# A weight ring of five chunks, a later load of key and value, and four chunks moved, in an attention and two-layer MoE kernel

## The chip, the cores and the metric

The kernel runs on one core of a Trainium2 chip. The metric is the time of one execution on the device in microseconds (us). The core has TensorE (PE, matmuls), VectorE (DVE), ScalarE (ACT), GpSimd (POOL, here only an issuer of DMAs) and SyncE (SP, the main issuer of DMAs). Each takes its own instructions in a fixed order, so an instruction that waits holds up all that stand behind it on its engine.

## The reference

```
a     = softmax over m of phi                     # phi: 4 batches, 8 heads, 576 tokens, 32 memories
k_m   = a^T k ;  v_m = a^T v                      # 32 memories of 64 per head
attn  = softmax(q k_m^T / 8) v_m                  # per head; then heads side by side: 512 per token
h     = relu(x @ w_in)                            # layer 1: 512 -> 2048
y     = (h * h) @ w_out                           # 2048 -> 512
h2    = y @ w_in2                                 # layer 2: 512 -> 2048
out   = (h2 * tanh(softplus(h2))) @ w_out2        # 2048 -> 512
```

There are 2304 tokens, 576 in each of 4 batches. The four weight matrices come in as 64-bit floats.

## The kernel before, in words

**Weights.** A *chunk* is 128 rows of 512 weights as pairs of 32-bit words, 512 KB. It is converted on the core: a Prelu on ACT works on the high words (line 197 in layer 1, 295 in layer 2), then a shift and a merge on DVE (lines 213 and 215, or 312 and 314) make 32-bit floats. Most operands are then split into a rounded *high* part (ACT) and the rest, the *low* part (DVE), and each product takes three matmuls: high by high, low by high, high by low. Layer 1 has 32 chunks (`i1` for w_in, `o1` for w_out, class `Conv`), layer 2 also 32 (`i2`, `o2`, class `Fold`).

**Conv.** `order` is the list of layer 1's chunks. `load` issues a chunk's load on SP into a raw tile that `spots` names: chunks 0 to 17 use nine places, six of them lent by other tiles, from chunk 18 on three. Ten chunks are begun in a script written out by hand at the start (line 659 on, with `strict(True)`: every engine keeps the order of the program). After that `tick` is called once per f: it begins one chunk on ACT, makes the bits of the one begun a tick ago, and the high and low parts of the one before it. `bits` calls `load` for a later chunk, when its raw tile is done with. `after` names the instruction behind which the DVE part is ordered; where it is set, that part is also behind the last emptying of a sum (`marks["ys"]`).

**Layer 1.** v_m is multiplied into w_in once per batch, so that layer 1 works on the softmax's weights: 32 matmuls of 64 rows (line 514) make two *pages* of the product, `wp`; for batches 2 and 3 w_in comes back from DRAM (`load_page`, line 947). `a_tile` (line 600) is the main loop: for one half batch of 288 tokens and a range of f (16 blocks of 128 of the 2048), six matmuls make h (lines 613 to 615), ACT takes ReLU and square (624, 625), ACT or DVE the high part (629, 631), DVE the low part (632), and, three f later, twelve matmuls add into four sums in PSUM (575 to 577). After the last f, `evac_y1` empties the sums (590, 592, 594). One f is 18 matmuls. Batches 0 and 1 are done in three groups of f, 0 to 3, 4 to 7, 8 to 15, each for four half batches (`subs`, numbered 0 to 11; 0 and 1 are in the script), because the weights arrive meanwhile. Then come batch 2's halves and batch 3's halves with all 16 f each.

**Fold.** Layer 2 is computed with seven products for eight; `Fold` makes their operands from pairs of chunks: per pair two Prelu, two shifts, two merges, four sums and seven casts (ACT high, line 331; DVE low, 332), each of which POOL stores (333). `fold.tick` begins a chunk every second or third f and takes one step of a pair, two where more than four wait. `fold.cap` (26, `EARLY`) is how many chunks are taken before batch 3; what is left of them is run off in a `while fold.busy()` loop after batch 2, and the rest goes to batch 3's f. The cast tiles rotate over the idle places of other tiles: first over that of k and v (`kv`, as `parts`), in batch 3 over those (`ru`) that later take layer 2's operands.

**Key and value.** k and v of one half of the heads are one tile with one buffer (`kv`). `kv_unit` makes the memories in five steps; after the first two, `kv_later` leaves n idle f (1 for batch 2), in which the next k and v land.

**Order.** Where no `issue_after` or `behind` binds, a planner with its own model of times sets the order on each engine, mostly by the program's order.

Of the kernel before, what the change touches and what calls it, by code (L numbers as in the profile page):

```python
# [18 lines left out]
P = 128  # L19
# [13 lines left out]
ROLE = [0, 1, 2, 3, 0, 2, 3]  # L33
EARLY = 26

# [22 lines left out]
def body(tc, q, kvm, kvt, phi, w_in1, w_out1, w_in2, w_out2, out):  # L58
# [41 lines left out]
    kv_t, kt_t, q_t = {}, {}, {}  # L100

    def load_phi(b, p):
        sp.dma_start(phi_t[p][:, at[p]:at[p] + S], phi[b, p])

    def load_kv(b, p):

        t = Y.tile([P, 2, 4, NC, D], F32, tag="kv", name=f"kv{b}{p}", bufs=1)
        sp.dma_start(
            t.rearrange("p s g c d -> p s (g c d)"), kvm[b, p].rearrange("s p x -> p s x"))
        kv_t[b, p] = t  # L110
# [49 lines left out]

    marks = {}

    @contextlib.contextmanager
# [8 lines left out]
    class Conv:  # L172


        def __init__(self, order, spot, ready=lambda key, u: True):
            self.order, self.spot, self.ready = list(order), spot, ready
            self.loaded = self.started = 0
            self.limit, self.after, self.paced, self.hold = len(self.order), None, False, False
            self.raw, self.flight, self.done = {}, [], set()

        def load(self, n=1):
            for _ in range(n):
                if self.loaded == len(self.order):
                    return
                key, u = self.order[self.loaded]
                pool, tag, bufs = self.spot(self.loaded)
                t = pool.tile([P, 512, 2], I32, tag=tag, name=f"raw_{key}_{u}", bufs=bufs)
                src = w_v[key][u] if key[0] == "i" else w_v[key][:, u, :]
                sp.dma_start(t.rearrange("p o t -> p (o t)"), src)
                self.raw[key, u] = t  # L190
                self.loaded += 1
# [9 lines left out]
        def bits(self, x, place=None):  # L201
# [16 lines left out]
            if key == "i1" and c:  # L218
                nc.gpsimd.dma_start(w1[u // 2], wt["i1", u // 2])
            self.raw.pop((key, u))  # L220
            if not self.hold:
                self.load()
# [42 lines left out]
    class Fold:  # L265


        def __init__(self, order):
            self.order = list(order)
            self.cap = len(self.order)  # L270
            self.loaded = self.started = 0
            self.raw, self.bits, self.odd, self.steps = {}, [], {}, []
            self.pool, self.stage, self.n = None, None, 0

# [14 lines left out]
        def tick(self, start=True):  # L289
            todo, self.bits = self.bits, []  # L290
            if start and self.started < self.loaded and len(self.steps) < 5:
                key, u = self.order[self.started]
                high = self.raw[key, u][:, :, 1].bitcast(F32)
                with behind(marks, "step"):
                    act.activation(high, high, AF.Prelu, scale=2.0 ** -112, alpha=-2.0 ** 32)
                self.started += 1
                self.bits.append((key, u))
            with behind(marks, "step"), behind(marks, "low"), behind(marks, "ys"):
                for key, u in todo:
                    self.fields(key, u)  # L300
                for _ in range(2 if len(self.steps) > 4 else 1):
                    if self.steps:
                        self.steps.pop(0)()
# [277 lines left out]
    def evac_y1(b, half, first, last):  # L581
        slot = 2 * b + half if b < 2 else half

        def f(dm, o):
# [6 lines left out]
            elif dm % 2 == 0:  # L591
                act.copy(st, o)
            else:
                marks["ys"] = vec.tensor_copy(st, o)
# [52 lines left out]
    for f0, f1 in zip(bounds, bounds[1:]):  # L647
# [4 lines left out]
        for f in range(f0, f1, 2):  # L652
            order.append(("o1", f))
            if f + 2 < f1:
                order += [("i1", f + 2), ("i1", f + 3)]
            order.append(("o1", f + 1))
    spots = [(Y, "raw", 3)] * 3 + [
        (wo, f"wo{part}{j}", 1) for j in (7, 6, 5) for part in "hl"]

    c1 = Conv(order, lambda i: spots[i % 9 if i < 18 else i % 3],  # L660
              lambda key, u: key != "i1" or u < 8 or (1, u // 2 - 4) in wp)
# [99 lines left out]
    bits(1)  # L761
    first_h(0, 0)
    ps = banks2("pw001")[:, :, :P]
    w_mm([ps[:, p] for p in range(2)], 0, 0, P, 2 * P)
    act.copy(plain[0][:, :, P:], ps)
    relu(0, 0)
# [92 lines left out]
    first_a(1, 3)  # L859
    first_y(1)  # L860
    bits(9)
    c1.low(conv[6])
    c1.low(conv[7])
    strict(False)
# [7 lines left out]
    def kv_later(b):  # L872
# [10 lines left out]

        n = 1 if b == 2 else 4
        return [[u, 2], [iter(range(n)), n], [u, 3]]

    def counted(u, counts):
        for n in counts:
            for _ in range(n):
                next(u)  # L890
            yield

# [57 lines left out]
    for i, (f0, f1, b, half) in enumerate(subs):  # L950
# [3 lines left out]
        if i == 2:  # L954
            c1.after, c1.paced = "first", True
            lanes = [[counted(at11, (2, 1, 2)), 3]]
        elif i == 3:
            drain(lanes)
            c1.after = (1, 1)
        elif i == 4:  # L960
            c1.after = None
        elif i == 8:
# [3 lines left out]
        elif final:  # L966
            drain(lanes)
            lanes = [[iter(range(2)), 2]] + attn_later(2, 0)
            for j in range(4):
                load_page(j)  # L970

        def tick(fc):
            if len(c1.done) < 2 * NF:
                c1.tick(start=(i, fc) != (2, 0))

# [86 lines left out]
    cm_cv, CV = open_pool("cv", "right")  # L1062
    fold.pool = CV
    def stage_cv(n):
# [321 lines left out]
```

## Time and profile before

| | us |
|---|---|
| median of 3 runs | 744.89 |
| lowest, highest | 744.54, 745.78 |
| profiled execution, whole | 745.91 |
| profiled execution, span | 744.1 |
| PE, DVE, ACT busy | 726.7 (98%), 524.0 (70%), 419.7 (56%) |
| chain that ended last | PE 83%, DMA 8%, DVE 4%, ACT 3% |

The span is what the profiler saw between the first and the last instruction. An engine's busy time is the time in which at least one of its instructions ran; matmuls overlap, so a busy PE is not PE at its peak. Idle time of PE is what can be saved, as far as nothing else takes its place. The granted clock of PE is full throughout.

### The profile page before, as it was taken

What the parts mean: (1) busy time and instruction counts of PE and PEld (TensorE: products, weight loads), DVE (VectorE), ACT (ScalarE), POOL (GpSimd) and SP (SyncE); (2) the same over time, 40 slices, a digit from 0 to 9 for tenths busy, and PEclk for the clock granted to TensorE, in tenths of its full rate; (3) what the DMA queues carried; (4) which work ended last, traced back from release to release, by engine and by line L of the source; (5) the groups of instructions that cost most, each with busy time, mean ns of one, the idle gap of its engine ahead of it and who ended that gap; (6) DMA issues with size and microseconds to landing.
All of it is one profiled execution on the core that took longest, in us unless ns stands there. A gap on an engine that the chain in (4) does not pass through costs nothing.

```text
span 744.1 us, 16262 instructions
## 1 busy us (share of the span) xinstructions
PE 726.7 (98%) x5990; PEld 696.5 (94%) x5990; DVE 524.0 (70%) x1117; ACT 419.7 (56%) x957; POOL 66.7 (9%) x128
## 2 busy tenths in 40 slices
PE   8998998999999999999999999999999999999998
PEld 7677997998989989899999999999999999999998
DVE  4879867655777798969556767955667873666574
ACT  3767867774777687857435336533435552434552
POOL 0000000221212232424100000000000000000000
PEclk9999999999999999999999999999999999999999
DMA  8994554589898588767829889898978788778882
GB/s 331 406 353 142 199 168 144 204 300 343 281 333 303 192 294 302 281 244 269 306 90 331 258 289 322 262 293 272 315 248 268 244 289 267 271 230 270 248 267 71
DMA packets 89327, 195.33 MB, mean 262 GB/s; under 512 B 9888, under 2 KB 22688, under 8 KB 89248
## 3 DMA queue, kind: packets, MB, share of 16 engines
q1 hardware_dynamic: 78992, 160.60, 64.3%
q0 software_dynamic: 10112, 33.56, 11.8%
q8 instruction: 48, 0.79, 0.4%
q14 instruction: 31, 0.25, 0.1%
q10 hardware_dynamic: 144, 0.13, 0.1%
HBM read 151.26 MB, written 42.99 MB: 261 GB/s over the span
## 4 chain that ended last, share of the span: by engine, by line
PE 83%; DMA 8%; DVE 4%; ACT 3%; issue 1%; SPq 1%; DVEq 0%; ACTq 0%
PE hb L1186 8%; PE hb L1187 8%; PE hb L1188 8%; PE a L575 6%; PE a L577 6%; PE a L576 6%; DMA raw_o<-in_moe_w_out_dram 3%; PE h L613 3%; PE h L614 3%; PE h L615 3%; DMA raw_i<-in_moe_w_in_dram 2%; PE a L53 2%; DMA kv<-in_kvm_dram 1%; DMA kv01v<-in_kvm_dram 1%; PE h L53 1%
## 5 line engine op out<-in xcount | busy, mean ns | idle before, releaser
L575 PE MATMUL a<-g,o1h 128*128 128x288 f32 x480 | 140.6, 298 | 5.5 <-DVE ys L590 3.6
L576 PE MATMUL a<-g,o1l 128*128 128x288 f32 x480 | 139.3, 295 | 0.0
L577 PE MATMUL a<-g,o1h 128*128 128x288 f32 x480 | 128.6, 297 | 0.6 <-DVE g L632 0.6
L1187 PE MATMUL hb<-ycl,u 128*128 128x384 f32 x336 | 112.9, 336 | 0.0
L1186 PE MATMUL hb<-ych,u 128*128 128x384 f32 x336 | 112.9, 336 | 0.0
L1231 DVE TENSOR_TENSOR opl<-a,oph 128x384 fp32r<-128x384 f32 x144 | 79.1, 556 | 45.3 <-ACT oph L1230 44.7
L1188 PE MATMUL hb<-ych,u 128*128 128x384 f32 x336 | 109.4, 336 | 0.0
L1230 ACT CAST oph<-a 128x384 fp32r<-128x384 f32 x144 | 73.9, 513 | 58.8 <-PE b20b L1254 7.0
L575 PEld LDWEIGHTS a<-g,o1h 128*128 128x128 f32 x480 | 90.2, 188 | 9.2 <-DVE ys L590 3.5
L1192 ACT ACTIVATE a<-hs 128x384 f32<-128x384 f32 x72 | 37.8, 526 | 97.4 <-DVE hs L1196 97.4
L576 PEld LDWEIGHTS a<-g,o1l 128*128 128x128 f32 x480 | 90.4, 188 | 0.2 <-issue 0.2
L577 PEld LDWEIGHTS a<-g,o1h 128*128 128x128 f32 x480 | 85.6, 188 | 1.7 <-DVE g L632 1.3
L624 ACT ACTIVATE s<-h 128x288 f32<-128x288 f32 x120 | 49.1, 410 | 60.9 <-PE h L615 55.9
L613 PE MATMUL h<-ah,wp 128*128 128x288 f32 x240 | 72.8, 304 | 1.7 <-ACT s L624 0.8
L614 PE MATMUL h<-al,wp 128*128 128x288 f32 x240 | 70.9, 296 | 0.5 <-DVE al L506 0.5
L632 DVE TENSOR_TENSOR g<-s,g 128x288 fp32r<-128x288 f32 x120 | 54.3, 453 | 23.7 <-ACT g L629 22.7
L615 PE MATMUL h<-ah,wp 128*128 128x288 f32 x240 | 70.6, 296 | 0.0
L1196 DVE TENSOR_TENSOR hs<-hu,hb 128x384 f32<-128x384 f32 x72 | 39.8, 553 | 41.1 <-PE hb L1188 40.5
L1186 PEld LDWEIGHTS hb<-ych,u 128*128 128x128 f32 x336 | 63.1, 188 | 0.0
L1187 PEld LDWEIGHTS hb<-ycl,u 128*128 128x128 f32 x336 | 63.0, 188 | 0.0
L1188 PEld LDWEIGHTS hb<-ych,u 128*128 128x128 f32 x336 | 62.8, 188 | 0.0
L625 ACT ACTIVATE s<-s 128x288 f32<-128x288 f32 x120 | 52.9, 446 | 0.9
(358 smaller groups left out, 1707.4 us busy)
## 6 DMA issues: line engine op xcount, KB each, us to landing
u<-wf_i SPq DMA_DIRECT2D x168, 256.0 KB, 4.0
u<-wf_o SPq DMA_DIRECT2D x168, 256.0 KB, 3.3
raw_i<-in_moe_w_in_dram SPq DMA_DIRECT2D x32, 512.0 KB, 6.6
raw_o<-in_moe_w_out_dram SPq DMA_DIRECT2D x32, 512.0 KB, 5.3
wf_i<-st POOLq DMA_DIRECT2D x41, 256.0 KB, 4.5
wf_o<-st POOLq DMA_DIRECT2D x39, 256.0 KB, 4.6
win1r<-w_i SPq DMA_DIRECT2D x16, 512.0 KB, 6.3
kv<-in_kvm_dram SPq DMA_DIRECT2D x5, 1024.0 KB, 6.9
```

The costliest lines, as they stand in the source:

```text
L575: pe.matmul(o, wh[:, c, cs], sh, start=first, stop=False)
L576: pe.matmul(o, wl[:, c, cs], sh, start=False, stop=False)
L577: done_pe["main"] = pe.matmul(o, wh[:, c, cs], sl, start=False, stop=last)
L613: pe.matmul(ph, w[:, 0, hg, fs], hi[:, hg], start=(hg == 0), stop=False)
L614: pe.matmul(ph, w[:, 0, hg, fs], lo[:, hg], start=False, stop=False)
L615: done_pe["h"] = pe.matmul(ph, w[:, 1, hg, fs], hi[:, hg], start=False, stop=(hg == 1))
L632: marks["low"] = vec.tensor_sub(sl, s, sh.bitcast(F32))
L1186: pe.matmul(ps, wh, yh[:, d], start=(j < 4 and d == 0), stop=False, **kw)
L1187: pe.matmul(ps, wh, yl[:, d], start=False, stop=False, **kw)
L1188: pe.matmul(ps, wl, yh[:, d], start=False, stop=end, **kw)
L1230: marks["s"] = act.copy(hi, x)
L1231: marks["v"] = sub(lo, x, hi.bitcast(F32))
```

## The change

- **The ring (`spot`, `load`).** From layer 1's chunk 18 on there are five raw tiles instead of three: two of every five are halves of a tile `pair` in the place of k and v. A chunk from number 20 on is loaded when not more than four are loaded ahead of the one to be converted next (`taken + 5`).
- **The order of `Conv`.** `after` stays `"first"` for all tiles, which is now the end of batch 1's last softmax; before, it was dropped from tile 4 on. Conversions begin at the third f of tile 2, not at the second.
- **The script.** The steps of batch 1's second softmax (`at11`) stand in the script, between the conversions' lows and bits; before, they were a lane of tiles 2 and 3. `first_h(0, 0)` stands behind the matmuls of the second piece of the product.
- **Key and value.** Two idle f for batch 2 instead of one. The first four `load_page` of batch 2 are issued behind the last load of k and v.
- **Fold.** `EARLY` is 22 instead of 26, so ten chunks instead of six are left to batch 3, where two steps are taken as soon as more than two wait. Its Prelu and its steps are also ordered behind ACT's copies of the sums (`ysa`).

```diff
-EARLY = 26
+EARLY = 22
-        sp.dma_start(
+        marks["kv"] = sp.dma_start(
...
-                if self.loaded == len(self.order):
+                if self.loaded == len(self.order) or self.loaded >= max(20, self.taken + 5):
                     return
                 key, u = self.order[self.loaded]
-                pool, tag, bufs = self.spot(self.loaded)
-                t = pool.tile([P, 512, 2], I32, tag=tag, name=f"raw_{key}_{u}", bufs=bufs)
+                t = self.spot(self.loaded, f"raw_{key}_{u}")
...
             self.raw.pop((key, u))
+            self.taken += 1
...
-                with behind(marks, "step"):
+                with behind(marks, "step"), behind(marks, "ysa"):
                     act.activation(high, high, AF.Prelu, scale=2.0 ** -112, alpha=-2.0 ** 32)
...
-            with behind(marks, "step"), behind(marks, "low"), behind(marks, "ys"):
+            with behind(marks, "step"), behind(marks, "low"), behind(marks, "ys"), behind(marks, "ysa"):
                 for key, u in todo:
                     self.fields(key, u)
-                for _ in range(2 if len(self.steps) > 4 else 1):
+                for _ in range(2 if len(self.steps) > self.deep else 1):
...
-                act.copy(st, o)
+                marks["ysa"] = act.copy(st, o)
...
-    c1 = Conv(order, lambda i: spots[i % 9 if i < 18 else i % 3],
+    pair = []
+
+    def spot(i, name):
+        if i >= 18 and i % 5 < 2:
+            if not pair:
+                pair.append(Y.tile([P, 2, 512, 2], I32, tag="kv", name="pair", bufs=1))
+            return pair[0][:, i % 5]
+        pool, tag, bufs = spots[i % 9 if i < 18 else 0]
+        return pool.tile([P, 512, 2], I32, tag=tag, name=name, bufs=bufs)
+
+    c1 = Conv(order, spot,
...
-    first_h(0, 0)
     ps = banks2("pw001")[:, :, :P]
     w_mm([ps[:, p] for p in range(2)], 0, 0, P, 2 * P)
+    first_h(0, 0)
...
     first_y(1)
+    next(at11)
+    next(at11)
+    c1.low(conv[6])
+    next(at11)
+    c1.low(conv[7])
+    next(at11)
     bits(9)
-    c1.low(conv[6])
-    c1.low(conv[7])
+    next(at11)
...
-        n = 1 if b == 2 else 4
+        n = 2 if b == 2 else 4
...
             c1.after, c1.paced = "first", True
-            lanes = [[counted(at11, (2, 1, 2)), 3]]
-        elif i == 3:
-            drain(lanes)
-            c1.after = (1, 1)
-        elif i == 4:
-            c1.after = None
+            lanes = []
...
-            for j in range(4):
-                load_page(j)
+            with behind(marks, "kv"):
+                for j in range(4):
+                    load_page(j)
...
-                c1.tick(start=(i, fc) != (2, 0))
+                c1.tick(start=i > 2 or fc > 1)
...
-    fold.pool = CV
+    fold.pool, fold.deep = CV, 2
```

## Rows read from the trace of the kernel before

**Rows 1.** Waits of PE, 50 to 120: waiter, awaited, total us, times, longest

```profile
PE a L575 <- DVE ys L590: 3.6, 3, 2.4
PE a L577 <- DVE g L632: 0.6, 1, 0.6
PE h L614 <- DVE al L506: 0.5, 1, 0.5
PE h L613 <- ACT wp L520: 0.5, 1, 0.5
```

**Rows 2.** Waits of PE, 120 to 386

```profile
PE pk L427 <- DMA kv<-in_kvm_dram: 1.5, 1, 1.5
PE a L575 <- ACT g L629: 1.2, 2, 1.0
PE h L613 <- ACT s L624: 0.8, 1, 0.8
PE a L575 <- ACT ys L592: 0.7, 1, 0.7
```

**Rows 3.** Timeline of PE: start, us, instruction, [idle before it, releaser]

```profile
116.47 0.40 PE L575 MATMUL a<-g,o1h 128*128 128x288 f32 x1 [2.38 <-DVE ys L590]
```

**Rows 4.** Timeline of DVE

```profile
101.06 0.43 DVE L213 TENSOR_SCALAR win<-raw_i 128x512 int32<-128x512 int32 x1 [4.24 <-DMA raw_i<-in_moe_w_in_dram]
...
102.38 0.45 DVE L590 TENSOR_TENSOR ys<-a,ys 128x288 f32<-128x288 f32 x1
```

**Rows 5.** Waits of SP, 60 to 118

```profile
SPq L189 <- DVE ct_o L215: 34.2, 6, 16.5
```

**Rows 6.** The page, part 6: DMA issues, count, size, median us to landing

```profile
u<-wf_i SPq DMA_DIRECT2D x168, 256.0 KB, 4.0
...
raw_i<-in_moe_w_in_dram SPq DMA_DIRECT2D x32, 512.0 KB, 6.6
```

**Rows 7.** Chain that ended last, 163 to 200: start, us, what

```profile
170.65 10.91 DMA kv<-in_kvm_dram
...
198.63 1.02 PE pw20p L514 x32
```

**Rows 8.** Timeline of SP's issues

```profile
169.83 0.42 SPq L947 DMA_DIRECT2D win1r<-w_i  x1
```

**Rows 9.** Timeline of ACT

```profile
306.12 0.68 ACT L295 ACTIVATE raw_o<-raw_o 128x512 f32<-128x512 f32 x1 [2.66 <-DMA raw_o<-in_moe_w_out_dram]
```

**Rows 10.** Stretches: us, busy of each engine (instructions), clock, DMA share, GB/s

```profile
54.00:66.00 12.00, 10.93 (x75) 9.91 (x74) 11.72 (x27) 8.86 (x22) 0.53 (x1) 1.00 0.54 181
...
96.00:118.00 22.00, 18.43 (x157) 16.96 (x156) 13.06 (x29) 14.05 (x32) 0.53 (x1) 1.00 0.55 190
...
150.00:182.00 32.00, 30.48 (x316) 28.54 (x318) 17.98 (x45) 20.62 (x52) 6.55 (x13) 1.00 0.91 324
...
344.00:366.00 22.00, 22.00 (x167) 22.00 (x166) 14.14 (x40) 10.89 (x31) 5.34 (x10) 1.00 0.84 301
366.00:386.00 20.00, 20.00 (x147) 20.00 (x146) 13.73 (x24) 9.87 (x19) 0.00 (x0) 1.00 0.30 103
```

**Rows 11.** Timeline of DVE: a pair of layer 2's chunks

```profile
286.28 0.69 DVE L314 SCALAR_TENSOR_TENSOR raw_o<-raw_o 128x512 int32<-128x512 int32 x1
...
287.25 0.42 DVE L340 TENSOR_TENSOR raw_o<-ct_o 128x256 f32<-128x256 f32 x1
287.58 0.42 DVE L341 TENSOR_TENSOR raw_o<-raw_o,ct_o 128x256 f32<-128x256 f32 x1
```

**Rows 12.** Timeline of DVE: the last low part of layer 2's first operands

```profile
377.86 0.95 DVE L1090 TENSOR_TENSOR ycl<-yr,ych 128x768 fp32r<-128x768 f32 x1
```

**Rows 13.** Timeline of PE in the script

```profile
22.27 1.24 PE L53 MATMUL h<-at,plain 128*128 128x288 f32 x4 [0.53 <-ACT plain L53]
```

**Rows 14.** Timeline of DVE: a softmax pass, and the first low of g

```profile
54.10 0.75 DVE L484 TENSOR_TENSOR x<-x,smx 128x576 f32<-128x576 f32 x1
...
59.40 0.45 DVE L632 TENSOR_TENSOR g<-s,g 128x288 fp32r<-128x288 f32 x1
```

More of the change, by code (lines that the diff above doesn't have):

```diff
@@ L100, in body @@
     kv_t, kt_t, q_t = {}, {}, {}
+    marks = {}
     def load_phi(b, p):
@@ L159, in body @@
     wf = {key: dram.tile([NPG, P, 7, 512], F32, name=f"wf_{key}") for key in ("i2", "o2")}
-    marks = {}
     @contextlib.contextmanager
@@ L176, in __init__ @@
             self.order, self.spot, self.ready = list(order), spot, ready
-            self.loaded = self.started = 0
+            self.loaded = self.started = self.taken = 0
             self.limit, self.after, self.paced, self.hold = len(self.order), None, False, False
@@ L272, in __init__ @@
             self.raw, self.bits, self.odd, self.steps = {}, [], {}, []
-            self.pool, self.stage, self.n = None, None, 0
+            self.pool, self.stage, self.n, self.deep = None, None, 0, 4
         def load(self, n=1):
@@ L882, in kv_later @@
         u = lazy(lambda: kv_unit(b, "b0", nxt))
-        n = 1 if b == 2 else 4
+        n = 2 if b == 2 else 4
         return [[u, 2], [iter(range(n)), n], [u, 3]]
[L887 to L891, printed above, removed]
     def soft_both(b):
```

## The prediction

> **What bounds the kernel now.** I read the profile's page first: TensorE (PE) is busy for 98% of the span (the table above). Its busy time counts matmuls that overlap, so the share says only that little is left, not where. The list of waits of PE, asked for 50 to 120 us and for 120 to 386 us, gives the rest: 5.2 us in the four largest of the first stretch and 4.2 us in the second [rows 1, 2]; no wait of PE for another engine is listed after 386. So a gain can come only from these 9.4 us and from the script before 50 us. The longest gap of all, 2.38 us, stands at 116.47 [rows 3].
>
> Then I asked who is late in each gap.
>
> *The ring.* PE waits there for VectorE (DVE) to empty a sum (line 590). DVE is not short of time: it stands in its queue before a chunk's bits (line 213) until the chunk lands, 4.24 us at 101.06, and the sum's add comes two instructions later, at 102.38 [rows 4]. The chunk is late because its load went out late: SyncE (SP) stood before a load until DVE had converted an older chunk for 34.2 us in six waits, 16.5 us the longest [rows 5]. There are three raw buffers, and each load waits for the chunk three places ahead. A load takes 6.6 us in the median [rows 6]; a conversion is started once per f, and an f has 18 matmuls of about 0.13 us, 2.4 us. Counted in the program, a load with three buffers is released two f (4.8 us) before its chunk is started: too little for 6.6.
>
> *k and v.* Near 181.7 PE waits 1.5 us [rows 2] for a load issued at 170.65 that took 10.91 us [rows 7]; two page loads had gone out just ahead of it, the last at 169.83 [rows 8].
>
> *The drain.* ScalarE (ACT) waits 2.66 us for a raw chunk at 306.12 [rows 9]; behind it stand a ReLU and the copies that free the sums, and PE loses 0.8 + 0.7 us [rows 2].
>
> **The change part by part.** All terms are microseconds of the profiled span (744.1; 1.8 lie around it, and that run is 1.0 above the median of the three runs). I apply the sum to the median.
>
> (1) Five raw buffers and the order on DVE. With five, a load is released four f ahead (9.6 us against 6.6). I counted the ticks of both programs: the count of chunks started is one behind from the second f of batch 1's first half to the fourth f of batch 0's second half in the next group (a start is dropped), then equal, because the wait for batch 1's pages had cost one there anyway; so layer 1's last chunk and layer 2's first are started in the same f as before. Besides, the conversions' DVE work is now always ordered behind the last emptying of the sums (before, only in the first group), so a late chunk no longer stands ahead of that add, except in the first two f of a tile. The gap is 3.6 in three pieces [rows 1]. It is hidden afterwards by DVE and DMA time that is there: DVE is busy 13.06 of 22 us in this stretch, DMA 0.55 [rows 10]. I keep 0.4 for a chunk that still lands late: **-3.2** (0 to -3.6).
>
> A rule that speaks against it: the rows show DMA at 0.55 and 190 GB/s here, against 0.91 and 324 GB/s at 150 to 182 [rows 10]. The Trainium skill, page DMA: Bandwidth & Descriptors, section Issuing engines are not separate DMA queues, says that all DMAs interleave on the same 16 engines, wherever they are issued. By that rule two more loads in flight lengthen each other, and the term would be 0; by the row there is room, and the term is -3.2.
>
> (2) One more idle f before k and v of batch 2's second half are used (2.4 us against a wait of 1.5), and the first four page loads behind batch 3's k and v: **-1.5** (-1.5 to 0). What it moves on SP: the pages wait with everything behind them until PE is done with the old k and v, about 184 (one f later than today, less the wait) instead of up to 169.83. First use was at 198.63 [rows 7], so 14 us are left for about 3 MB at the 324 GB/s of the stretch [rows 10], 9 us: **+0.2** (0 to +2).
>
> (3) Four chunks go to batch 3. By the count of ticks, batch 2 ended with four chunks not yet started and ran them all in one drain; now it ends with the seven steps of one pair. The burst of casts on ACT and the loads within it go: **-1.0** of 1.5. I keep 0.5 because batch 3's first chunk waits for its load on ACT in the same way (bounds -1.5 to +0.5).
>
> The price stands in batch 3. A pair costs DVE two shifts, two merges (0.69), four sums and seven lows; thirteen of 0.42 and two of 0.69 are 6.8, and at the spacing of the rows (0.33 from start to start) 5.7 [rows 11]. Batch 3 takes five pairs, not three; two pairs, 11 to 14 us of DVE, come anew, of which I give back one pair, 5.7, as an estimate: today the drain holds the raw tiles, so batch 3's first pairs start late and run on into the last tile. DVE has 7.9 us free at 344 to 366 and 6.3 at 366 to 386 [rows 10]. So it fits, but the last pair (started at the ninth and eleventh f of the last tile) meets the operands of layer 2, whose last cast stood at 377.86 [rows 12], and moves it to about 383.5, when PE still has sums to finish until 386. The cast tiles of that pair are also those in which layer 2's first loads land; now some come free only near 380. I take **+0.8** (0 to +6.8: one pair's whole DVE time on the path).
>
> (4) Layer 2's casts on ACT now behind the copies of the sums. The waits of PE for ACT's g are 1.2 in two pieces [rows 2]; the first two f of a tile come before the copies in the program and are not caught: **-0.4** (0 to -1.0).
>
> (5) The first h behind the second piece of the product: PE waited 0.53 for ACT's copy at 22.27 [rows 13], and the h would fill it if the product's weights are ready before, which no row of a wait contradicts: **-0.3** (-0.5 to +0.5; a plus if the weights come later than I think and h stands behind them).
>
> (6) Batch 1's last softmax into the script. Its first pass of 0.75 stood at 54.10 [rows 14], and now waits for a copy, 0.6. Five such passes on DVE and two on ACT, taken alike (5.3), with two lows and one chunk's bits between (2.4, of which 1.5 lie beside ACT) and small steps (0.5), end near 61.3. That frees the wait of 0.5 for its last pass (line 506) [rows 1]. But in the script nothing is put ahead of it: the first g's low (line 632) stood at 59.40 [rows 14] and comes after it, and PE, which waited 0.6 for it, waits about 2.5. The wait of 0.5 for ACT's page cast (line 520) stays. -0.5 and +1.9, less 0.5 because one conversion less is started here: **+0.9** (-1.1, both waits gone, to +2.5).
>
> Sum: -3.2 - 1.5 + 0.2 - 1.0 + 0.8 - 0.4 - 0.3 + 0.9 = **-4.5**. 744.9 - 4.5 = **740.4**; in a profile like the one shown, a span of about 739.6.
>
> **The rivals.**
>
> *Everything is freed* (0.09): terms at their good ends, 3.6 + 1.5 + 1.5 + 1.0 + 0.5 + 1.1 = 9.2, gives 735.7; half way to it is 738.1. For: all gaps have cover. Against: DVE is busy for 11.72 of 12 us at 54 to 66 [rows 10], so (6) can hardly give all.
>
> *The ring is bound by transfers, not by buffers* (0.11): DMA loads of the same stretch get longer as more are in flight, term (1) is 0 and the rest stands: 744.9 - 1.3 = 743.6; with half of (1) 742.0. Against: DMA 0.55 there [rows 10]. The Trainium skill's rule named under (1) speaks for this case. The same number comes out if the longer ring does not do what it says, because the loads are still issued late: two extra buffers with a limit of five beyond the chunks taken.
>
> *Batch 3 takes it back* (0.08, slower): the last pair slips past the last tile. Then its 5.7 of DVE, its stores (taken as long as the loads) and the loads of layer 2 that wait for its tiles (4.0) [rows 6] come one after another from 377 on, to 391; PE has sums for until about 382, so about 9 are lost. The rest gives -5.3, so 744.9 + 3.7 = 748.6. It decides from a wait of 6.8 us on (5.3 + 1.5). For: DVE has 14 us free in the last tile and the added work is of that size. Against: by the count, the last chunk is started with five f to go.
>
> *In between* (0.07): batch 3 or the script costs 3 to 5 more than taken, 743.5 to 745.
>
> **How the numbers follow.** My forecast has 0.65 and holds 737.5 to 743.0. The range is 737.0 to 743.8: all of the forecast, half of the first rival and nearly all of the second, 0.80 together. About 0.2% (1.5 us, what a measurement of this kernel can tell from none) divides the signs: faster means below 743.4. Faster: 0.65 + 0.09 + 0.06 of the second rival = 0.80. Within: 0.05 of the second, 0.07 of the last and 0.01 of the third = 0.13. Slower: 0.07 of the third.
>
> **What would show it.** Of PE's waits, the 3.6 on line 590 and the 1.5 on k and v should be gone, and DVE's waits for raw chunks under 1 us each at 75 to 118; SP's raw loads evenly spaced from 76 on. ACT should not wait for raw chunks near 305. PE's first wait for line 632 should be longer than 0.6, and none for batch 1's casts after it. Between 366 and 390 PE should lose less than 1.5; more there, or new waits for pages near 195, would make the prediction wrong upward. If layer 1's last chunk is not converted earlier than 118, step (1) is wrong.

## The result, and the profile after

The changed kernel takes **736.69 us** (median of four executions, 736.37 to 738.81), the kernel before 745.34 beside it on the same chip; the ratio is 0.9889, with a 95% interval of 0.9865 to 0.9912. Measured once more on another chip it took 736.83 against 745.41 (0.9877, 0.9855 to 0.9900). The forecast was 740.4 with a range of 737.0 to 743.8: the sign is right, the gain is nearly twice the sum (8.6 against 4.5), and the median lies 0.3 below the range's low end, close to the rival "everything is freed" (735.7).

The profiled execution took 738.81 (span 737.0), the longest of the four; the second one 736.38 (span 734.5). They differ by the script before 55 us (1.55) and by one wait at the head of layer 2 (1.7 against 0.6 us), and by nothing between, so both are used below.

Waits of PE after, at 50 to 120, at 120 to 376 and from 376 to the end (waiter, awaited, total us, times, longest), which answer to [rows 1, 2]:

```profile
PE a L575 <- ACT g L629: 0.9, 1, 0.9
PE h L613 <- ACT s L624: 0.2, 1, 0.2
...
PE a L575 <- ACT g L629: 1.2, 2, 1.0
...
PE hb L1190 <- DMA u<-wf_i: 1.7, 1, 1.7
```

The 3.6 for the sums, the 0.6 + 0.5 + 0.5 around the softmax, the 1.5 for k and v and the 0.8 + 0.7 of the drain are gone; 0.9 at the first tile's start and 1.7 at the head of layer 2 are new; the 1.2 for g has stayed.

The timeline of DVE after, where [rows 4] showed 4.24 us of standing before a chunk:

```profile
97.84 0.46 DVE L590 TENSOR_TENSOR ys<-a,ys 128x288 f32<-128x288 f32 x1 [1.48 <-PE a L577]
98.22 0.45 DVE L632 TENSOR_TENSOR g<-s,g 128x288 fp32r<-128x288 f32 x1
98.58 1.18 DVE L590 TENSOR_TENSOR ys<-a,ys 128x288 f32<-128x288 f32 x3
99.68 0.45 DVE L632 TENSOR_TENSOR g<-s,g 128x288 fp32r<-128x288 f32 x1
100.05 0.76 DVE L212 TENSOR_SCALAR ct_o<-pair 128x512 int32<-128x512 int32 x2
```

All four sums (line 590) are emptied first, the chunk's bits (line 212, from the new buffer `pair`) come behind them, and DVE now waits for PE, not for a transfer. SP, however, waits as it did in [rows 5]:

```profile
SPq L188 <- DVE ct_o L214: 33.6, 6, 16.2
```

Five buffers do not make SP issue evenly: it still stands before a load until DVE has merged an older chunk (line 214), for as long as with three. So the row from which the prediction read that loads go out late looks the same without the gaps. What five buffers change is how early a load stands against its use. The stretch of 96 to 118 us in [rows 10], after (by 114 us PE has done about as many matmuls, 161 against 157):

```profile
96.00:114.00 18.00, 18.00 (x161) 17.30 (x160) 14.29 (x34) 15.08 (x36) 0.53 (x1) 1.00 0.72 247
```

PE is busy throughout; the DMA share rose from 0.55 to 0.72 and the rate from 190 to 247 GB/s. On the page, the raw loads of the one kind stand as

```profile
raw_i<-in_moe_w_in_dram SPq DMA_DIRECT2D x31, 512.0 KB, 7.3
```

against 6.6 in [rows 6], both for the whole run. Of those loads that go out from 60 to 118 us, before:

```profile
DMA to landing us min/median/max: 3.1/5.0/6.5
```

and after:

```profile
DMA to landing us min/median/max: 3.2/5.9/8.8
```

So loads did take longer, 0.9 us in the median, and PE has no wait for them. The Trainium skill, page DMA: Bandwidth & Descriptors, section Issuing engines are not separate DMA queues, says that all DMAs run on the same 16 engines and interleave there. The longer loads agree with it.

**The time by stage.** I cut each profile at four matmuls that every kernel has: the first h after the script (line 613; the expectations below call it the first h of the second group), and the first matmul of the weight pages `pw06p`, `pw26p` and `pw36p` (line 514). The first two in the second profile of the changed kernel:

```profile
53.07 0.51 PE L613 MATMUL h<-ah,wp 128*128 128x288 f32 x1
...
118.48 1.09 PE L514 MATMUL pw06p<-win,vT 64*32 64x256 f32 x32
```

| kernel | script, to first h | to pw06p | to pw26p | to pw36p | to the end | median us | ratio to before [95%] |
|---|---|---|---|---|---|---|---|
| before | 53.89 | 72.08 | 103.03 | 69.81 | 445.29 | | |
| changed | 54.62 | 65.40 | 101.71 | 69.84 | 445.43 | 736.69 | 0.9889 [0.9865, 0.9912] |
| changed, again | 53.07 | 65.41 | 101.71 | 69.86 | 444.45 | 736.83 | 0.9877 [0.9855, 0.9900] |
| ring3 | 53.77 | 67.03 | 101.81 | 69.84 | 444.55 | 740.81 | 0.9912 [0.9895, 0.9929] |
| order_old | 52.69 | 65.82 | 101.78 | 69.84 | 444.17 | 737.31 | 0.9864 [0.9848, 0.9881] |
| ring3_order_old | 54.04 | 69.74 | 101.74 | 69.84 | 445.24 | 743.71 | 0.9951 [0.9932, 0.9969] |
| kv_old | 53.23 | 65.42 | 102.37 | 69.83 | 444.35 | 737.56 | 0.9888 [0.9867, 0.9910] |
| pages_only | 53.95 | 65.47 | 101.71 | 69.82 | 444.45 | 737.17 | 0.9878 [0.9850, 0.9905] |
| early26 | 53.36 | 65.41 | 101.72 | 69.80 | 444.21 | 736.91 | 0.9864 [0.9846, 0.9882] |
| early26_no_ysa | 53.75 | 65.47 | 101.71 | 69.86 | 444.71 | 737.31 | 0.9877 [0.9855, 0.9900] |
| soft_old | 53.04 | 66.96 | 101.72 | 69.82 | 443.86 | 737.52 | 0.9889 [0.9866, 0.9912] |
| h_old | 53.28 | 65.41 | 101.71 | 69.84 | 443.96 | 735.79 | 0.9858 [0.9833, 0.9883] |
| every_f | 54.73 | 65.41 | 101.72 | 69.84 | 443.70 | 736.16 | 0.9871 [0.9847, 0.9894] |
| feed9_t13 | 53.91 | 65.47 | 101.71 | 68.57 | 442.74 | 734.54 | 0.9849 [0.9822, 0.9876] |

The three middle columns repeat to 0.1 us wherever nothing was edited, so an edit in such a stretch can be read there to a tenth, where the medians, with a script that moves by 2 us from one execution to the next, cannot tell 0.5 from nothing. From before to after they give -6.68 for the part right behind the script, -1.32 for the part with k and v, and 0; the last column, which holds the drain, batch 3 and layer 2, gives -0.8 to +0.1. Where loads come late a stretch need not repeat, and each kernel has one profiled execution: those of ring3 and ring3_order_old are the fastest and the second fastest of six, 2.0 and 1.4 under their medians.

### The profile page after: what moved, and what is told of

The parts are those of the page before. It is cut to its first block, busy times and chain, and to the rows that moved or that the text cites. A ratio compares the mean times of both kernels' runs of the same rounds, so it can differ in the third digit from the quotient of the medians.

```text
span 737.0 us, 16247 instructions
## 1 busy us (share of the span) xinstructions
PE 724.1 (98%) x5990; PEld 695.4 (94%) x5990; DVE 525.6 (71%) x1117; ACT 419.6 (57%) x957; POOL 65.9 (9%) x128
## 4 chain that ended last, share of the span: by engine, by line
PE 94%; DMA 2%; ACT 2%; SPq 1%; issue 0%; DVE 0%
PE a L575 9%; PE a L577 8%; PE a L576 8%; PE hb L1190 8%; PE hb L1192 8%; PE hb L1191 8%; PE h L613 4%; PE h L614 4%; PE h L615 4%; PE a L53 2%; DMA kv<-in_kvm_dram 1%; PE h L53 1%; DMA u<-wf_i 1%; PE b13acc L1258 1%; PE b03acc L1258 1%; PE b23acc L1258 1%
```

## The experiments

All are edits of the changed kernel, and "undone" means put back as it was before. ring3, order_old, ring3_order_old and early26 ran beside each other on one chip (the kernel before took 747.21 there), the changed kernel again with kv_old, soft_old and every_f on a second (745.41), h_old, pages_only and feed9_t13 on a third (746.10), early26_no_ysa on a fourth (745.95).

**The changed kernel again** (no edit).

> The changed kernel once more, nothing edited, as the measure for the three kernels beside it. 736.2 to 738.0. If the script before 50 us and the first weights of layer 2 are what differs from run to run, PE's waits between 120 and 376 come out as in the first profile (1.2 us on line 575 in two pieces), and the wait for u at the head of layer 2 lies anywhere from 0.2 to 1.7 us.

736.83; the stretches between 53 and 290 us are the same to 0.02, and the wait for u was 0.6. What varies is the script and the head of layer 2, as expected.

### The ring, and the order on DVE

**ring3**: three buffers, no limit.

```diff
-        if i >= 18 and i % 5 < 2:
-            ... (the two halves of pair)
-                if self.loaded == len(self.order) or self.loaded >= max(20, self.taken + 5):
+                if self.loaded == len(self.order):
```

> The changed kernel (736.7) with layer 1's last fourteen chunks in three raw buffers again and no limit on the loads; the order on VectorE stays. Theory 'buffers': three buffers release a load two f before its chunk is started (4.8 us against loads of 6.6), so the waits for the emptying of the sums (line 590) come back in 75 to 118, 3 to 3.6 us in three or so pieces, and the time rises by 3 to 4.5, to 739.7 to 741.2. Rival 'order': the gap came from conversions that stood ahead of the sums' adds in VectorE's queue; with the order kept, late chunks cost only their own matmuls: less than 1 us of waits, 736.4 to 737.7.

**order_old**: five buffers, the old order from the second group of layer 1 on.

```diff
+        elif i == 4:
+            c1.after = None
```

> The changed kernel (736.7) with five raw buffers, but from the fourth group of layer 1's half tiles on the conversions on VectorE are not ordered behind the emptying of the sums. Theory 'buffers': chunks are there in time, so nobody stands in VectorE's queue, and the time stays within 0.7, 736.2 to 737.4; PE's waits on line 590 at 75 to 118 are under 0.7. Rival 'order': 2 to 3.6 us of PE's waits on line 590 come back, 738.7 to 741. Third: both are needed, and each undone alone costs about 2.

**ring3_order_old**: both edits.

> The changed kernel (736.7) with both the three raw buffers and the old order on VectorE: term (1) of the prediction undone as a whole. Both theories: the 3.6 us of the kernel before come back, in three pieces; if a visible gap costs no more than its idle time, the time rises by 3.6 to 740.3; if each gap costs about 0.27 more than its idle (the last matmul's tail and the slower restart), by 4.4 to 741.1. Against it, 'bound by transfers': under 737.5.

To `pw06p` the three take 67.03, 65.82 and 69.74, against 65.41: +1.62, +0.41 and +4.33. In the medians ring3 (740.81, where "buffers" had put it) stands 3.5 above order_old, and both together 6.4 above it: more than the profiled executions show, and no trace says where. "Order" as a full explanation falls: with five buffers the old order costs 0.4. Counted matmul by matmul from the first h, even this 0.4 arises between 66 and 71 us, where the 32 matmuls of a page run in two pieces; behind it order_old keeps step with the changed kernel, although DVE stands 2.1 us before one chunk (75 to 118):

```profile
DVE ct_o L212 <- DMA pair<-in_moe_w_out_dram: 2.1, 1, 2.1
```

"Buffers" alone is too simple as well: with three, the order saves another 2.7, and the profile of ring3 lists only 0.5 of waits for the sums where 3 to 3.6 were expected. The two cover each other: buffers make chunks punctual but for that one, the order makes a late chunk cheap. DVE with three buffers, first with the old order (ring3_order_old), then with the new (ring3):

```profile
112.52 0.43 DVE L212 TENSOR_SCALAR ct_o<-raw_o 128x512 int32<-128x512 int32 x1 [1.40 <-DMA raw_o<-in_moe_w_out_dram]
112.86 0.81 DVE L590 TENSOR_TENSOR ys<-a,ys 128x288 f32<-128x288 f32 x2
```

```profile
110.84 1.54 DVE L590 TENSOR_TENSOR ys<-a,ys 128x288 f32<-128x288 f32 x4
112.31 0.75 DVE L212 TENSOR_SCALAR ct_o<-raw_o 128x512 int32<-128x512 int32 x2
```

In the first the add that frees a sum stands behind a chunk that has not landed; in the second it goes ahead.

The +4.33 of ring3_order_old is more than its gaps: 0.26 and 2.10 us of waits for the sums. The timeline of PE says where the rest went:

```profile
110.98 0.29 PE L615 MATMUL h<-ah,wp 128*128 128x288 f32 x1
113.37 0.61 PE L575 MATMUL a<-g,o1h 128*128 128x288 f32 x1 [2.10 <-DVE ys L590]
113.78 0.44 PE L576 MATMUL a<-g,o1l 128*128 128x288 f32 x1
114.02 0.44 PE L577 MATMUL a<-g,o1h 128*128 128x288 f32 x1
...
116.64 0.29 PE L576 MATMUL a<-g,o1l 128*128 128x288 f32 x1
116.77 0.29 PE L577 MATMUL a<-g,o1h 128*128 128x288 f32 x1
```

After the gap the next thirteen starts lie 0.41 and then 0.22 to 0.25 apart instead of 0.13, 1.56 us more in all. The stretches of that profile (us, busy of PE, PEld, DVE, ACT and POOL, granted clock, DMA share, GB/s) show the granted clock at half, its 1.2 GHz level, and back at 1 from 116.6:

```profile
114.00:115.00 1.00, 1.00 (x6) 1.00 (x6) 1.00 (x4) 0.69 (x2) 0.00 (x0) 0.50 0.00 0
115.00:116.00 1.00, 1.00 (x6) 1.00 (x6) 1.00 (x4) 0.78 (x2) 0.00 (x0) 0.50 0.67 156
...
117.00:118.00 1.00, 1.00 (x10) 1.00 (x9) 0.94 (x3) 0.83 (x3) 0.00 (x0) 1.00 0.78 168
```

From start to start, the two gaps are 2.26 and 0.50 more than the usual spacing; with the 1.56 that is 4.32, the whole of the +4.33. In the profile of before that the prediction read, the clock stayed at 1 after its gap of 2.38 [rows 3, 10]. But the mean clock that each execution lists was 0.998 or less in 30 of 36 executions of the kernel before and in 4 of 6 of ring3_order_old, and 0.999 or more in all 6 of ring3 and in 46 of 47 of the kernels with five buffers. (The one at 0.949, an execution of early26 of 738.7, has no explanation here.) Of those 36, the six with a clock of 1 have a median of 745.2, the thirty others 746.5, and on each of the four chips those with a clock of 1 lie below the median of the others. So the gap on the sums seems usually to cost some 1.3 us more than the profiled execution showed. That this comes from that one gap is shown by a trace for ring3_order_old alone; for the kernel before it is argued from the clocks.

### k, v and the pages

**kv_old**: used one f sooner, pages bound to nothing. **pages_only**: used one f sooner, pages still held.

```diff
-        n = 2 if b == 2 else 4
+        n = 1 if b == 2 else 4
-            with behind(marks, "kv"):       (kv_old only)
-                for j in range(4):
-                    load_page(j)
+            for j in range(4):
+                load_page(j)
```

> The changed kernel (736.7) with the keys and values of batch 2's second half used one f sooner again and the first four page loads bound to nothing: term (2) undone. Theory: the load of k and v still goes out behind the last use of the old ones and behind pages, takes about 11 us, and is used 2.4 us too soon for that: PE waits 1.3 to 1.7 us for kv near 176, and the time rises by 1.3 to 2.0, to 738.0 to 738.7. Rival: in the faster kernel the load goes out earlier against its use, or the ring's loads are out of its way, so nothing waits: 736.5 to 737.0.

> The changed kernel (736.8) with k and v of batch 2's second half used one f sooner again, but with the first four page loads still held behind batch 3's k and v: one half of term (2) alone. Theory 'the pages were in the way': with the pages held, the load of k and v issued near 163 lands in 6 to 7.5 us (against 10.3 with the pages ahead of it), before the use at about 172.8, so PE waits under 0.3 for it, and the time is 736.3 to 737.0: the additional idle f bought nothing by itself. Rival 'the f was needed': the load takes 9 to 10.5 us again, PE waits 0.6 to 1.0 near 173.7, and the time is that with both undone, 737.3 to 737.8.

From `pw06p` to `pw26p`: 102.37 for kv_old, 101.71 for pages_only, 101.71 changed. With the pages held the idle f buys nothing more; holding them buys all of the 0.66. Two idle f without held pages were not run, so whether the f alone would have done as well is open. SP's issues and PE's wait in kv_old, and the landing times of its two loads of k and v (min/median/max):

```profile
161.56 0.33 SPq L955 DMA_DIRECT2D win1r<-w_i  x1
161.98 0.41 SPq L597 DMA_DIRECT2D y<-ys  x1
162.49 0.42 SPq L955 DMA_DIRECT2D win1r<-w_i  x1
163.30 0.38 SPq L110 DMA_DIRECT2D kv<-in_kvm_dram  x1
...
173.69 0.54 PE L427 MATMUL pk<-kv,et 128*32 128x128 f32 x12 [0.85 <-ACT s L625]
...
DMA to landing us min/median/max: 7.4/8.8/10.3
```

and in pages_only, where the pages follow at 175.62:

```profile
164.07 0.37 SPq L110 DMA_DIRECT2D kv<-in_kvm_dram  x1
...
175.62 2.35 SPq L955 DMA_DIRECT2D win1r<-w_i  x4
...
DMA to landing us min/median/max: 6.5/7.2/7.9
```

163.30 + 10.3 = 173.6 is when PE goes on, although the wait is put down to ACT. The wait is thus for the load. Two pages of 512 KB had gone out 0.8 and 1.7 us ahead of it, as in [rows 7, 8]; with the pages held it lands in 7.9. This agrees with what the Trainium skill, page DMA: Bandwidth & Descriptors, section Issuing engines are not separate DMA queues, says of the 16 engines.

### Batch 3 and the head of layer 2

**early26**: 26 chunks before batch 3 (and the pace there as before).

```diff
-EARLY = 22
+EARLY = 26
-    fold.pool, fold.deep = CV, 2
+    fold.pool, fold.deep = CV, 4
```

> The changed kernel (736.7) with 26 chunks of layer 2 converted before batch 3 instead of 22, and the quicker pace in batch 3 taken back: term (3) undone. Theory 'batch 3 takes part of it back': the drain's 1.5 us of waits at 300 to 310 return and cost 1.5 to 2.3, and the 1.7 us in which TensorE waits for layer 2's first weights at 396 goes, with what stands around it (2.1 in all): net -0.6 to +0.4, 736.1 to 737.1, and the wait for u on line 1190 is under 0.3. Rival 'batch 3 has room': the wait at 396 has another cause and stays, and the time rises by 1.5 to 2.3, to 738.2 to 739. A third, that the drain's end costs nothing: 734.6.

From `pw36p` to the end 444.21, against 444.45 and 445.43 of the changed kernel and 445.29 before. From `pw36p` to batch 3's last matmul on the sums (line 577) early26 takes 87.02, the kernel before 88.11, and the nine kernels with 22 chunks and the pace of the change 86.13 to 86.14; from there to the end 357.19, 357.18, and 357.7 to 359.3. So moving four chunks wins 0.9 in the drain and costs 0.5 to 2.1 afterwards: net about nothing, as the theory said, or a loss. In early26 the drain has one wait, and none for u is listed:

```profile
PE a L575 <- ACT ys L592: 0.7, 1, 0.7
```

SP's queue differs at the head of layer 2 (352 to 400, changed kernel again; in early26 the line is not there):

```profile
SPq L1135 <- DMA wf_o<-st: 15.0, 5, 10.4
```

Loads of layer 2's weights wait for the stores of the last casts, whose tiles they take. Of the nine profiles with 22 chunks and the pace of the change, two list no wait of PE for u, the others 0.2 to 1.7. That PE waits because of the stores is not shown: the two that list no wait (soft_old, h_old) have the line with 17.3 and 14.8 us.

**early26_no_ysa**: the same, and layer 2's casts on ACT no longer behind the copies of the sums.

```diff
-                with behind(marks, "step"), behind(marks, "ysa"):
+                with behind(marks, "step"):
-            with ..., behind(marks, "ys"), behind(marks, "ysa"):
+            with ..., behind(marks, "ys"):
```

> The changed kernel with 26 chunks of layer 2 before batch 3, as in the run of that name (there the drain cost one wait of 0.7 us on line 592, and the stretch from the last page of weights, pw36p, to batch 3's last matmul on the sums 87.0 us; in the kernel before 1.5 us in two waits, and 88.1), and layer 2's casts on ACT no longer held behind the copies of the sums: terms (3) and (4) undone together. Theory 'the order on ACT halves the drain's price': the second wait, 0.8 us for ACT's s on line 624 or so, is back and the stretch takes 87.8 to 88.2. Rival 'the order does nothing': one wait of 0.7 and 87.0 as before, and what the kernel before lost more there came from its raw chunk that landed late. In both the wait of 1.0 us for g at the start of batch 2's second half tile stays at 0.9 to 1.2, since what stands there comes before the copies in the program.

Both fell. In the drain a wait of 0.2 is left instead of 0.7, and from `pw36p` to batch 3's last matmul on the sums the kernel takes 86.76 instead of 87.02, so the order on ACT costs a little there rather than saving 0.8; the 1.0 for g in batch 2 stays, as expected. The drain's waits of 0.8 + 0.7 are thus nearly gone with both terms undone, although ACT still stands for a raw chunk nearly as long as in [rows 9]:

```profile
302.60 0.70 ACT L295 ACTIVATE raw_o<-raw_o 128x512 f32<-128x512 f32 x1 [2.27 <-DMA raw_o<-in_moe_w_out_dram]
```

It stands there behind the copies and before the next ReLU, not between a ReLU and its square as in the kernel before. Of the 1.97 by which the changed kernel is shorter here than the kernel before, 1.35 came with neither term; which part of the change brought it is not shown. And PE waited 0.5 for u although the last casts were long over: the stores of batch 3 are not the only reason for that wait. What else delays u there stays open.

**every_f**: layer 2's conversions in batch 3 are started in every f with room.

```diff
     def tick3(fc):
-        fold.tick(start=fc % 2 == 0)
+        fold.tick()
```

> The changed kernel (736.7) with layer 2's conversions in batch 3 started in any f that has room, not in every other: by the program's order the last cast then stands in the third f of the second half, not in the sixteenth. Theory: what batch 3 gives back is the wait of layer 2's first weights for the tiles of the last pair's casts; with the casts over by then, TensorE's wait for u goes (under 0.2 us) and the stretch from the last matmul of batch 3 on the sums to the end is 357.2, as in the kernel before: 734.6 to 735.9. Rival: the denser work on VectorE delays its sums and casts in batch 3's first half, 300 to 340, by 1 to 3 us of PE's waits on lines 575 and 613: 736.5 to 738.5. Third: the wait for u has another cause and stays, 736.7.

736.16, 0.7 under the changed kernel beside it, less than the intervals tell apart; to the end 443.70 from `pw36p`. No new wait arises in 300 to 345, so the rival fell, but the wait for u is 0.5, not gone: half of the theory.

### The softmax and the first h

**soft_old**: batch 1's last softmax spread over the next two half tiles again.

```diff
+            lanes = [[counted(at11, (2, 1, 2)), 3]]
```

> The changed kernel (736.7) with batch 1's last softmax passes spread over the first half tiles of layer 1's second group again: term (6) undone. Theory 'waits counted by the trace': the waits of 0.5 for its last pass and of 0.5 for ACT's page cast return and the 0.9 for g at the tile's start shrinks to 0.6; with what each gap costs beyond its idle (about 0.27), 1.0 to 2.3 more between the first h of that group and the fourth page of weights (65.4 us in the changed kernel), 737.7 to 739.0. Rival, the prediction's own term: the first g is made sooner when five passes do not stand before it, and the time falls by 0.5 to 0.9, to 735.8 to 736.2, with the first h of that group 0.5 to 1 earlier.

To `pw06p` 66.96 against 65.41: +1.55, the theory's side. From the first matmul on the script's last page (tile `pw10mm`, at 48.27) to the first h at 53.04 it is 4.77 us, as in every kernel here, so the five passes in the script cost PE nothing there. PE's waits at 50 to 120:

```profile
PE a L577 <- DVE g L632: 0.7, 1, 0.7
PE h L613 <- ACT wp L520: 0.4, 1, 0.4
PE h L614 <- DVE al L506: 0.3, 1, 0.3
```

Listed are 1.4, only 0.3 more than the 1.1 of the changed kernel, for 1.55 us. Two things are not in the list: each gap costs more than its idle time (next part), and two gaps, of 0.29 and 0.24 beyond the usual spacing (at 55.13 and 63.10), are missing from it, since the modelled end of the matmul ahead covers 0.16 of each and little is left.

**h_old**: the first h of layer 1 ahead of the second piece of the product.

```diff
+    first_h(0, 0)
     ps = banks2("pw001")[:, :, :P]
     w_mm([ps[:, p] for p in range(2)], 0, 0, P, 2 * P)
-    first_h(0, 0)
     act.copy(plain[0][:, :, P:], ps)
```

> The changed kernel (736.8) with the first h of layer 1 ahead of the second piece of the product again: term (5) undone. Theory 'the landings set the script': PE's wait of about 0.5 for the copy of plain near 22 returns, but the first h of the second group still stands at 52.7 to 54.7, where six kernels with one and the same script have it, and the median is 736.5 to 737.2. Rival 'the swap pays': the script is 0.5 to 0.9 longer, the first h of the second group stands beyond 53.9 and the median is 737.3 to 737.8.

The script, first h_old, then pages_only, which has the swap:

```profile
19.59 1.14 PE L53 MATMUL h<-at,plain 128*128 128x288 f32 x4
20.65 0.45 PE L53 MATMUL pw<-win,vT 64*32 64x128 f32 x16
21.63 1.24 PE L53 MATMUL h<-at,plain 128*128 128x288 f32 x4 [0.53 <-ACT plain L53]
```

```profile
20.52 0.45 PE L53 MATMUL pw<-win,vT 64*32 64x128 f32 x16 [0.60 <-DVE win L53]
20.90 2.21 PE L53 MATMUL h<-at,plain 128*128 128x288 f32 x8
```

The swap trades the 0.53 for a wait of the product for its weights, which the h used to cover. From the product's first piece (18.21 in h_old) to the first a (23.74) h_old takes 5.53 and the kernel before 5.52; the twelve profiles with the swap take 5.55 to 6.14. Neither theory had that sign: the swap costs 0 to 0.6. The median of 735.79 agrees, but it is from another chip than the changed kernel's.

### A version that goes further

**feed9_t13**: every_f; the first loads of layer 2's weights three f earlier; no conversion in the first two f of batch 2's second half.

```diff
-        if fc == 12:
+        if fc == 9:
             feed(8)
...
+            if half and fc < 2:
+                return
-            fold.tick(start=fc % 3 == 0)
+            fold.tick(start=fc in (2, 4, 7, 10, 13, 15) if half else fc % 3 == 0)
```

> The kernel with layer 2's conversions in batch 3 started in any f (736.2), with two edits more: the first eight loads of layer 2's weights go out three f earlier in batch 3's last half tile, and no conversion or cast is issued in the first two f of batch 2's second half tile. Theory: the 1.0 us that PE waits there for ACT's g near 255 comes from four casts that stand ahead of it and goes, which gives 1.0 to 1.3; the 0.5 us for layer 2's weights near 396 goes too, with 0.5 to 0.8: 734.0 to 734.9. Rival: the casts that are held back pile up at the end of batch 2, and PE waits 1 us or more at 295 to 305 instead: 735.5 to 737; and the loads of weights, sent earlier, push the loads of y behind them, with a wait of the same size for yr or yc.

**734.54**, ratio 0.9849 [0.9822, 0.9876], and after 120 us one wait is left in the list:

```profile
PE a L575 <- ACT g L629: 0.2, 1, 0.2
```

By the medians, from two chips, it cannot be told from every_f. By the stage it can: the stretch to `pw36p` takes 68.57 instead of 69.84 in every_f, -1.27, for one wait listed at 1.00. This is the wait in the changed kernel again:

```profile
253.89 0.29 PE L615 MATMUL h<-ah,wp 128*128 128x288 f32 x1
255.18 0.40 PE L575 MATMUL a<-g,o1h 128*128 128x288 f32 x1 [1.00 <-ACT g L629]
255.42 0.29 PE L576 MATMUL a<-g,o1l 128*128 128x288 f32 x1
```

Matmuls run 0.29 but start 0.13 apart. From start to start the gap is 1.29, 1.16 more than usual: the 0.16 by which the matmul ahead outlasts the spacing counts as busy. The next one follows after 0.24, not 0.13: another 0.11. **A listed wait of 1.00 costs 1.27**, and taking it away gave as much.

## Why the prediction was right or wrong

*What bounds the kernel.* Right as to place: every stretch that became shorter is one that the list of waits had named, and none other did. Wrong as to size: "a gain can come only from these 9.4 us" takes the listed idle for the loss. Nine of the eleven gaps went; at 0.27 more each that is 2.4 us, an estimate. Gaps of up to 0.3 can be missing from the list, and the clock after the longest gap comes on top where it falls.

*(1) Ring and order*, -3.2: **-4.33** by the profile of ring3_order_old, and 6.8 by its median against that of early26 beside it, which has the new ring and order. The mechanism is right: buffers and order together undone bring the waits for the sums back. The working of buffers against f is right only in part: 6.6 is the median of the whole run, while the loads of 60 to 118 us took 5.0 (`raw_i`, longest 6.5) and 3.4 (`raw_o`, longest 7.6), so that against 4.8 only the longer ones come late. The size is short by what each gap costs beyond its idle and, going by the mean clocks, in most executions by the clock. "DVE's waits for raw chunks under 1 us" came true (none of 0.2 or more is listed at 75 to 118), and layer 1's last chunk is merged at 116.6 (118.0 before); "raw loads evenly spaced" did not come true. The rival "bound by transfers" falls: those `raw_i` loads went from 5.0 to 5.9, and PE has no wait.

*(2) k and v*, -1.3 with the pages: **-0.66** for the edit undone in the changed kernel, -1.32 from before to after. Most of the other 0.66 is the load itself: issued 44.7 us after `pw06p` in both, it took 10.91 before and 10.3 in kv_old. The number holds, the reason is not borne out: the prediction gave the gain to the idle f and booked the held pages as a cost of +0.2, and the held pages alone take the wait away. It had the two page loads in front of it [rows 8] and did not ask what they did to the 10.91 of [rows 7]. No wait for pages followed near 195.

*(3) Four chunks to batch 3*, -0.2: **-0.3 to +1.2** by early26, of which -0.9 in the drain (-1.0 predicted) and +0.5 to +2.1 after it (+0.8). ACT's 2.66 for a raw chunk [rows 9] is now 0.2:

```profile
ACT raw_o L295 <- DMA raw_o<-in_moe_w_out_dram: 0.2, 1, 0.2
```

Both sizes were near. But the burst made at most a part of the drain's waits: with 26 chunks again they are 0.7, and without the order on ACT as well 0.2, not 1.5. The price came at the head of layer 2, where one of the two named mechanisms put it; that it comes by the tiles which the first loads take is not shown. The rival "batch 3 takes it back" falls: nothing like 9 us was lost.

*(4) ACT's casts behind the copies*, -0.4: **nothing gained** (with 26 chunks 0.3 lost in the drain; with 22 it was not undone). The 1.0 for g stands in the first f of a tile, before the copies in the program, which the prediction said and still booked 0.4. Holding the casts out of those f, as feed9_t13 does, takes the wait away.

*(5) The swap*, -0.3: **0 to +0.6**. The failed step is "which no row of a wait contradicts": no wait for those weights is listed before because an h covered it. The named bound of +0.5 was the better value.

*(6) The softmax*, +0.9: **-1.55**. The step that failed is that the first low of g would come 2 us later behind the passes in DVE's queue. The passes do end near the 61.3 that the prediction gave, but the first low goes ahead of the last of them (DVE, changed kernel again):

```profile
56.67 0.46 DVE L632 TENSOR_TENSOR g<-s,g 128x288 fp32r<-128x288 f32 x1
...
60.88 0.76 DVE L53 TENSOR_TENSOR al<-at,ah 128x576 fp32r<-128x576 f32 x1
```

In the first tile after the script PE waits 0.9 for ACT's g instead of 0.6 for the low, one wait in place of three. The bound of -1.1 was the better value, and too tight, again by what a gap costs beyond its idle.

*The sum.* By the stage readings -4.3 - 0.7 + 0.4 + 0.3 - 1.55 is about -5.8, with the middles of (3) and (5). From before to after three stretches give more than their parts undone one by one: 0.8 to `pw06p`, 0.7 with k and v, and 1.1 in the drain (88.11 against 87.02). With them it is about -8.4, and the rest of the 8.6 is within what the script and the head of layer 2 move from execution to execution. Of the 0.8, counted matmul by matmul, 0.65 arises within the first 160 matmuls after the first h (about 20 us), where the kernel before falls 2.2 behind the changed one and soft_old 1.6; the later start of the conversions falls into that stretch and was not undone by itself. The largest error of the sum is (6), 2.45 with the wrong sign; then come the 1.1 of (1) and the 1.1 in the drain. The low end of the range lies 3.4 below the sum, which leaves little room for an error that all gaps share, their price, beside a wrong sign. That the median lies close to "everything is freed" is in part luck: (4) and (5), which that rival counted with 1.5, gave nothing, and the stretch to `pw06p`, which it counted with 3.6 + 1.1, gave 6.7.

## What to carry to other kernels

Price a gap from start to start of the matmuls around it, never from the listed idle: here 0.27 us more each, and more still where the granted clock falls after it. One profiled execution may not show that; the mean clock of the others can hint at it. Before giving a late transfer more time, look at what was issued just ahead of it: here holding back the loads ahead of it took the wait away without more time. An order that moves work off a waiting PE must be checked for what that work had covered.

## What the runs showed of the hardware that I had not expected

After 2.10 us without a matmul TensorE's granted clock was 0.50 over 3.2 us of dense work (113.4 to 116.6 in ring3_order_old), while after 2.38 us in the profile of before and after 1.69 us in that of the changed kernel it stayed at 1.00. By the mean clocks, executions of the kernel before that lost it took about 1.3 us longer; no trace of that kernel shows one. And a load of 1 MB took 10.3 us with two loads of 512 KB up to 1.7 us ahead of it, at most 7.9 without them.
